# Folding the router's gate and noise weights into the MLP's second matrix, as 16 more columns, in place of transposes and products in the router

## The chip, the core and the metric

The kernel runs as one program on one core of a Trainium2 chip. The core has five engines that run their own instruction streams in order and meet only at semaphores: TensorE (PE, with its weight loads listed apart as PEld), VectorE (DVE), ScalarE (ACT), GpSimd (POOL) and SyncE (SP, which issues most DMA transfers). The metric is the device time of one execution in microseconds, as the median of several runs.

## The reference, cut to what matters

```python
# 1. linear attention over 3072 tokens: 4 batches x 8 heads x 768 steps, head size 48
state = alpha[t][:, None] * state + outer(k[t], v[t]);  y[t] = q[t] @ state
x = y as [3072, 384]
# 2. dense MLP
h = x @ w_in                       # [3072, 2048]
x = (h * sigmoid(h)) @ w_out       # [3072, 384]
# 3. mixture of experts, 8 experts, the best 2 for each token
logits = x @ w_gate;  noise_scale = log1p(exp(x @ w_noise))     # both [3072, 8]
noisy = logits + noise_scale * noise
# the two largest of noisy choose the experts, a softmax over the two weighs them
out[token] += weight * (relu(x[token] @ w1[e]) @ w2[e])
```

Since `x` of part 3 is `g @ w_out`, the two small products can also be written `g @ (w_out @ w_gate)` and `g @ (w_out @ w_noise)`. The change rests on that.

## The kernel before, in words

The program has three overlapping parts. The order of the instructions on each engine is the order in which the Python code issues them: nothing reorders them later.

**Attention** goes over 24 chunks of 128 tokens. `stage1_units` yields five units for a chunk: `unit_kt` with `unit_a` (transposes of k, products of k and q, masked on DVE into `am`), `unit_kv` (the state; DVE sums it in a tile `St` and scales it into `S`), two halves of `unit_y`, the second of which ends with the copy `xr` on ACT, and `unit_x` (transposes of `xr`, then `xh` on ACT and `xl` on DVE). Between them DVE prepares the next chunk (`prep_a`, `prep_b`, `prep_c`). All their PSUM tiles come from one pool `p1` with three buffers, name `ps1`, taken in turn.

**The MLP** goes over 8 blocks of 384 tokens (index `j`) and 16 slices of the hidden width (index `m`). `l1(j, m)` is 9 matmuls of 384 columns into a tile `ph`; `act1` makes `th` (ACT), `gf` (DVE), `gh` (ACT) and `gl`; `l2(j, m)` adds 9 matmuls into three accumulators `acc`, one for each 128 tokens. `l2` follows `l1` two iterations later (`LAG`). Matmuls run on pairs of high and low parts, three products for one. One attention unit is issued in each iteration, so the units of the first 15 yields stand alone at the start, and the other 105 lie between the MLP's matmuls.

**The MLP's weights** arrive in float64 halves. `narrow` turns a slice into float32 with three DVE instructions (lines 142 to 144) in a tile `wf` with three buffers, and `split` writes the high part on ACT (line 137) and the low part on POOL (line 138). `wn` and `wh` call them. Nine of the 32 slices are done in the first 15 units; in block 0 each iteration does two more, one of `wout` and one of `win`, until iteration 11. The high and low parts of `wout` are `wo_h` and `wo_l`.

**The router** of a block (`route(j)`) runs in steps between the iterations of the next block. For each of its three chunks it transposes the row of 384 values (3 PE transposes, line 96), copies them to `xt2` on ACT (line 531), multiplies by `wgn_t` (written as 3 matmuls of 16 columns, line 524; the trace counts 6) and copies the 16 sums beside the row (line 525). Then `gate` picks two experts on DVE, and POOL scatters the rows. The router of the last block runs in the first iterations of the expert part, which follows with its own matmuls (`e1`, `e2`).

Of the kernel before, what the change touches and what calls it, by code (L numbers as in the profile page):

```python
# [8 lines left out]
F32 = mybir.dt.float32  # L9
# [12 lines left out]
DM = H * D  # L22
# [32 lines left out]
def attention_mlp_moe(ctx: ExitStack, tc: tile.TileContext, aqk, vt, win, wout, wgn, noise, w12,  # L55
# [38 lines left out]
    def flip(o, x):  # L94
        n = x.shape[0]
        PE.transpose(o, x, ident[:n, :n])
# [21 lines left out]

    win_h = wpool.tile([128, MF, KD, 128], F32R)
    win_l = wpool.tile([128, MF, KD, 128], F32R)  # L120
    wo_h = wpool.tile([128, MF, DM], F32R)
    wo_l = wpool.tile([128, MF, DM], F32R)
    raw = {}

    def load_w(src, m):
# [10 lines left out]
    def split(h, l, r, eng=None):  # L136
        ACT.activation(h, r, AF.Copy)
        (eng or DVE).tensor_tensor(l, r, h.bitcast(F32), OP.subtract)
# [194 lines left out]
    def unit():  # L333
        next(gen, None)
# [19 lines left out]
    def wh(w):  # L354
        if w:
            (kind, m), f = w
            h, l = (win_h, win_l) if kind == "i" else (wo_h, wo_l)
            split(*[x[:, m].rearrange("p k j -> p (k j)") if kind == "i" else x[:, m] for x in (h, l)], f, POOL)

    wl(2)  # L360
    load_chunk(2)
# [5 lines left out]
    nc.scalar.dma_start(nz, noise)  # L367
    for i in range(15):
        unit()

    def range_load(i):
        raw["r", i] = load_w(win if i < MF else wout, i % MF)
# [69 lines left out]

    def l2(j, m):
        if m == 0:
            ACC[j] = [pa.tile([128, 512], F32, name=f"acc{i}")[:, :DM] for i in range(CPB)]
        gh, gl = GH.pop((j, m)), GL.pop((j, m))
        for i in range(CPB):
            sl = slice(i * C, (i + 1) * C)
            n = 0
            for g, w in ((gh, wo_h), (gh, wo_l), (gl, wo_h)):  # L450
                PE.matmul(ACC[j][i], g[:, sl], w[:, m], start=(m == 0 and n == 0),  # L451
                          stop=(m == MF - 1 and n == 2))
                n += 1
# [4 lines left out]
    def evac(j):  # L458
        rows[j] = r = rpool.tile([128, CPB, LGN], F32, name="row")
        for i in range(CPB):  # L460
            ACT.activation(r[:, i, :DM], ACC[j][i], AF.Copy, scale=0.5)
            if dbg is not None:
                c = j * CPB + i
                nc.sync.dma_start(dbg[c * C:(c + 1) * C], r[:, i, :DM])
# [52 lines left out]
    def route(j):  # L517
        c0 = j * CPB
        r = rows.pop(j)
        for i in range(CPB + 1):  # L520
            if i:
                p = p1.tile([128, 2 * E], F32, name="ps1")
                for k in range(KD):
                    PE.matmul(p, t[:, k], wgn_t[:, k], start=(k == 0), stop=(k == KD - 1))
                ACT.activation(r[:, i - 1, DM:], p, AF.Copy)
            if i < CPB:
                p = p1.tile([128, KD, 128], F32, name="ps1")
                for k in range(KD):
                    flip(p[:, k], r[:, i, k * 128:(k + 1) * 128])
                t = rpool.tile([128, KD, 128], F32, name="xt2")  # L530
                ACT.activation(t, p, AF.Copy)
            yield int(i < CPB) or None
        o, w, d = yield from gate(rpool, CPB, r[:, :, DM:DM + E], r[:, :, DM + E:], nz[:, c0:c0 + CPB])
        sel = rpool.tile([128, CPB, E], BF, name="sel")
        DVE.tensor_tensor(sel, o[:, :, 0], o[:, :, 1], OP.add)
        yield 1
        rk = p1.tile([128, CPB, E], F32, name="ps1")
        cb = cum[:, j % 2]
        PE.matmul(rk, tri, sel, start=True, stop=False)
        PE.matmul(rk, ones, cb[:, None, :].to_broadcast([128, CPB, E]), start=False, stop=False)  # L540
        for i in range(CPB - 1):
            n = CPB - 1 - i
            PE.matmul(rk[:, i + 1:], ones, sel[:, i:i + 1].to_broadcast([128, n, E]), start=False,
                      stop=i == CPB - 2)
        rs = rpool.tile([128, CPB, E], F32, name="rk")
        ACT.activation(rs, rk, AF.Copy)
        rk = rs
        cn = cum[:, (j + 1) % 2]
        DVE.tensor_reduce(cs, sel.rearrange("p c e -> p e c"), axis=AX.X, op=OP.add)
        DVE.tensor_tensor(cn, cb, cs, OP.add)  # L550
        DVE.tensor_copy(r[:, :, RW - 1].bitcast(I32), tok[:, c0:c0 + CPB])
        yield from gate_w(rpool, CPB, o, w, d, r[:, :, DM:DM + E])
        yield
        az, th = [rpool.tile([128, CPB, E], F32, name=x) for x in ("az", "rth")]
        ow = rpool.tile([128, CPB, 2, E], F32, name="ow")
        DVE.tensor_scalar(az, rk, float(CAP), 65536.0, op0=OP.is_ge, op1=OP.mult)
        DVE.tensor_tensor(th, rk, base, OP.add)
        DVE.tensor_tensor(th, th, az, OP.add)
        if j > PAST:
            DVE.tensor_scalar(az[:, :, :2], rk[:, :, :2], float(GRAB), 65536.0, op0=OP.is_lt, op1=OP.mult)  # L560
            DVE.tensor_tensor(th[:, :, :2], th[:, :, :2], az[:, :, :2], OP.add)
        DVE.tensor_tensor(ow, o, th[:, :, None, :].to_broadcast([128, CPB, 2, E]), OP.mult)
        pos = rpool.tile([128, CPB, 2], F32, name="pos")
        idx = rpool.tile([128, CPB, 2], I32, name="idx")
        DVE.tensor_reduce(pos, ow, axis=AX.X, op=OP.add)
        DVE.tensor_copy(idx, pos)
        yield
        scat[j] = []
        for i in range(CPB):
            for k in range(2):  # L570
                st = POOL.indirect_dma_start(
                    out=xd, out_offset=bass.IndirectOffsetOnAxis(ap=idx[:, i, k:k + 1], axis=0),
                    in_=r[:, i, :RW], in_offset=None, bounds_check=ROWS - 1, oob_is_err=False)
                for x in sum(scat.values(), []):
                    tc.declare_no_dep(st.ins, x.ins, reason="distinct rows")
                scat[j].append(st)
        assert bool(early) == (j > PAST)
        for st in scat[j]:
            for ld in early:
                tc.declare_no_dep(st.ins, ld.ins, reason="rows past those")  # L580
# [50 lines left out]
    for i in range(NS + LAG):  # L631
        if i < NS:
            j, m = divmod(i, MF)
            l1(j, m)
            if 12 <= i < 20:
                init_rows(i - 12, 8)
            if 32 <= i < 48 and i % 4 == 0:
                init_out(i // 4 - 8, 4)
            if 2 * MF <= i < 6 * MF:
                x = i - 2 * MF  # L640
                if x % 2 == 0:
                    range_load(x // 2)
                if x % 2 == 1 and x > 1:
                    range_check(x // 2 - 1)
            if i == 6 * MF:
                range_check(2 * MF - 1)
            if j == NB - 1:
                if m == 10:
                    okgen = ok_first()
                if m >= 10:  # L650
                    step(okgen)
                if m == 0:
                    s1c.close()
                    wev = w3c.enter_context(tc.tile_pool(name="wev", bufs=1, side="right"))
                    wst = w0c.enter_context(tc.tile_pool(name="wst", bufs=1, side="right"))
                    w3p[0], w3p["raw"] = wev, (wst, 2)
                if m == 1:
                    early = load_group(0, 0, wst, 4)
                if 8 <= m < 8 + len(GR[0][1]):
                    tr_tile(0, 0, m - 8)  # L660
                if m < 8:
                    w3_load(0, m)
                if m in (10, 11):
                    w3_load(1, m - 10)
                if 1 <= m < 9:
                    w3_split(0, m - 1)
            ac = act1(j, m)
            if j == 0:
                for _ in range(2):
                    w = wn()  # L670
                    step(ac)
                    wh(w)
                    step(ac)
            else:
                run(ac)
            if m < MF - 1 and j < NB - 1:
                unit()
        if i >= LAG:
            j, m = divmod(i - LAG, MF)
            l2(j, m)  # L680
            if m == MF - 1:
                evac(j)
            if m == 1 and j > 0:
                rgen = route(j - 1)
            for _ in range(LASTN if j == NB - 1 else 1 + (m >= RT2)):
                if rgen:
                    got = next(rgen, 0)
                    if got == 0:
                        rgen = None
                    if got == 1:  # L690
                        break
# [292 lines left out]
```

## Time and profile before

| what | value |
|---|---|
| median of 3 runs | 1103.37 us (1103.02 to 1105.49) |
| profiled execution, span from first to last instruction | 1103.1 us |
| PE busy | 1041.6 us, 94% of the span |
| DVE, ACT, POOL busy | 585.2, 399.6, 259.0 us |
| granted TensorE clock, mean | 0.987 |

The span and the median differ by 0.3 us. A PE that is 94% busy is not PE at its peak, since matmuls overlap and their ends are modelled. The share is also an average: in the first 130 us PE is busy less, and DVE more, than later. The sections below read those stages apart.

### The profile page before, as it was taken

The numbers are of one execution on the slowest core, as the hardware profiler recorded it, in microseconds if no ns is written. First come the engines' busy times: TensorE is split into PE (matmuls) and PEld (weight loads), VectorE is DVE, ScalarE is ACT, GpSimd is POOL, SyncE is SP. The second block draws the span as 40 slices with busy tenths as digits, with TensorE's granted clock in tenths as the row PEclk, the third lists the DMA queues.
The fourth block names the chain that finished last, engine by engine and source line by source line (L and its number), as shares of the span: only waits on it lengthen the run. The fifth ranks groups of instructions, "written<-read, shape, count | busy, mean of one in ns | idle before, by whom it ended". The sixth has DMA issues, their size and how long they took to land. (4 is left out here: it accounts for less than half of the span.)

```text
span 1103.1 us, 16832 instructions
## 1 busy us (share of the span) xinstructions
PE 1041.6 (94%) x6395; PEld 1006.9 (91%) x6395; DVE 585.2 (53%) x1319; ACT 399.6 (36%) x853; POOL 259.0 (23%) x252
## 2 busy tenths in 40 slices
PE   4678899999999999999999999999999999999995
PEld 3667799999999999999999998999999999999995
DVE  7889845657667676585646562244333333334220
ACT  3233343343433433334345431244333333333221
POOL 4455520310202102020020222211212122222212
PEclk9998899999999999999999999999999999999998
DMA  7344791533424224230032313545444344343212
GB/s 229 122 133 139 257 286 56 187 123 126 136 80 146 76 77 131 71 110 23 1 118 82 128 66 95 113 101 155 114 99 108 86 120 91 81 109 70 42 15 38
DMA packets 55225, 119.64 MB, mean 108 GB/s; under 512 B 6640, under 2 KB 33648, under 8 KB 55136
## 3 DMA queue, kind: packets, MB, share of 16 engines
q1 hardware_dynamic: 43456, 97.23, 28.4%
q0 software_dynamic: 11264, 20.68, 10.0%
q8 instruction: 52, 0.85, 0.3%
q10 hardware_dynamic: 416, 0.58, 0.2%
q14 instruction: 37, 0.30, 0.1%
HBM read 82.22 MB, written 36.24 MB: 107 GB/s over the span
## 5 line engine op out<-in xcount | busy, mean ns | idle before, releaser
L736 PE MATMUL acc<-w3h,hx 128*128 128x384 f32 x832 | 241.6, 342 | 1.9 <-ACT y L746 1.9
L717 DVE SCALAR_TENSOR_TENSOR hx<-ph,hx 128x64 fp32r<-128x64 f32 (+1 forms) x192 | 79.2, 443 | 295.6 <-ACT hx L713 293.0
L748 POOL DMA_INDIRECT out_dram<-y,xrow x64 | 98.5, 1539 | 335.0 <-ACT y L746 271.6
L713 ACT ACTIVATE hx<-ph 128x448 fp32r<-128x448 f32 (+1 forms) x128 | 65.5, 518 | 271.3 <-PE ph L710 191.8
L736 PEld LDWEIGHTS acc<-w3h,hx 128*128 128x128 f32 x832 | 153.1, 188 | 5.4 <-ACT y L746 2.2
L736 PE MATMUL acc<-w3l,hx 128*128 128x384 f32 x448 | 150.1, 335 | 0.0
L451 PE MATMUL acc<-wo_h,gh 128*128 128x384 f32 x384 | 139.5, 363 | 0.0
L710 PE MATMUL ph<-xh,w3h 128*128 128x384 f32 (+1 forms) x384 | 135.9, 354 | 0.8 <-DVE hx L717 0.8
L710 PE MATMUL ph<-xh,w3l 128*128 128x384 f32 (+1 forms) x384 | 135.1, 352 | 0.0
L710 PE MATMUL ph<-xl,w3h 128*128 128x384 f32 (+1 forms) x384 | 134.8, 351 | 0.0
L424 PE MATMUL ph<-xh,win_h 128*128 128x384 f32 x384 | 133.0, 346 | 1.2 <-DVE gf L434 0.6
L451 PE MATMUL acc<-wo_l,gh 128*128 128x384 f32 x384 | 130.1, 339 | 0.0
L451 PE MATMUL acc<-wo_h,gl 128*128 128x384 f32 x384 | 130.0, 339 | 0.0
L424 PE MATMUL ph<-xl,win_h 128*128 128x384 f32 x384 | 129.6, 337 | 0.0
L424 PE MATMUL ph<-xh,win_l 128*128 128x384 f32 x384 | 129.6, 337 | 0.0
L434 DVE SCALAR_TENSOR_TENSOR gf<-th,ph 128x384 f32<-128x384 f32 x128 | 70.5, 551 | 95.3 <-ACT th L431 84.6
L431 ACT ACTIVATE th<-ph 128x384 f32<-128x384 f32 x128 | 62.5, 488 | 134.7 <-PE ph L424 132.4
L439 ACT ACTIVATE gh<-gf 128x384 fp32r<-128x384 f32 x128 | 67.2, 525 | 112.3 <-DVE gf L434 108.6
L441 DVE TENSOR_TENSOR gl<-gf,gh 128x384 fp32r<-128x384 f32 x112 | 62.7, 559 | 66.3 <-ACT gh L439 62.8
L736 PEld LDWEIGHTS acc<-w3l,hx 128*128 128x128 f32 x448 | 81.1, 181 | 0.7
L451 PEld LDWEIGHTS acc<-wo_h,gh 128*128 128x128 f32 x384 | 73.6, 192 | 2.5
L710 PEld LDWEIGHTS ph<-xh,w3h 128*128 128x128 f32 x384 | 72.2, 188 | 3.8 <-DVE hx L717 1.1
(140 smaller groups left out, 1757.6 us busy)
## 6 DMA issues: line engine op xcount, KB each, us to landing
wraw<-in_w_dram SPq DMA_DIRECT2D x64, 384.0 KB
aqk<-in_aqk_dram SPq DMA_DIRECT2D x23, 674.2 KB
wraw<-in_win_dram SPq DMA_DIRECT2D x32, 384.0 KB
wraw<-in_wout_dram SPq DMA_DIRECT2D x32, 384.0 KB
xrow<-xd SPq DMA_DIRECT2D x48, 196.5 KB
xd<-pad SPq DMA_DIRECT2D x12, 589.5 KB
v<-in_v_dram SPq DMA_DIRECT2D x24, 192.0 KB
xd<-pad SPq DMA_DIRECT2D x4, 786.0 KB
```

What stands on the lines that cost most here:

```text
L424: PE.matmul(p, w[:, m, k], x[:, k], start=(n == 0), stop=(n == 3 * KD - 1))
L431: ACT.activation(th, p, AF.Tanh, scale=0.5)
L434: DVE.scalar_tensor_tensor(g, th, 1.0, p, op0=OP.add, op1=OP.mult)
L439: ACT.activation(gh, g, AF.Copy)
L441: (POOL if j == 0 else DVE).tensor_tensor(gl, g, gh.bitcast(F32), OP.subtract)
L451: PE.matmul(ACC[j][i], g[:, sl], w[:, m], start=(m == 0 and n == 0), stop=(m == MF - 1 and n == 2))
L710: PE.matmul(p[:, :N], w[:, k, fs], x[:, k], start=(n == 0), stop=(n == 3 * KD - 1))
L713: ACT.activation(hx[:, :N], p[:, :N], AF.Relu)
L717: DVE.scalar_tensor_tensor(hx[:, o:o + b - a], p[:, a:b], 0.0, hx[:, a:b].bitcast(F32), op0=OP.max, op1=OP.subtract)
L736: PE.matmul(AC3[e, g][t][:m], hx[:, o:o + m], w[:, f], start=(f == 0 and q == 0), stop=(f == FF - 1 and q == len(prods) - 1))
L748: st = POOL.indirect_dma_start(out=out, out_offset=bass.IndirectOffsetOnAxis(ap=x[:n, RW - 1:].bitcast(I32), axis=0), in_=y[a:a + n], in_o ...
```

## The change

Each slice of `wout`, once narrowed, is also multiplied by the gate and noise weights. `fold` transposes it (3 PE transposes), copies the result on ACT into a tile of the name `St`, multiplies by `wgn_t` on PE, copies the 16 columns into `wo_h` on ACT and subtracts into `wo_l` on DVE. It runs after units 5, 10 and 15 (for one, two and one slices), and once at the head of each iteration 1 to 12 of block 0, behind that iteration's `l1`. The matmuls of `l2` become 400 columns wide, the accumulators are copied with 400 columns, and the router loses its transposes and products.

```diff
-    wo_h = wpool.tile([128, MF, DM], F32R)
-    wo_l = wpool.tile([128, MF, DM], F32R)
+    wo_h = wpool.tile([128, MF, LGN], F32R)
+    wo_l = wpool.tile([128, MF, LGN], F32R)
...
+            if kind == "o":
+                folds.append((m, f))
+    folds = []
+    def fold():
+        while folds:
+            m, f = folds.pop(0)
+            p = p1.tile([128, KD, 128], F32, name="ps1")
+            for k in range(KD):
+                flip(p[:, k], f[:, k * 128:(k + 1) * 128])
+            t = s1.tile([128, KD, 128], F32, name="St", bufs=1)
+            ACT.activation(t, p, AF.Copy)
+            p = p1.tile([128, 2 * E], F32, name="ps1")
+            for k in range(KD):
+                PE.matmul(p, t[:, k], wgn_t[:, k], start=(k == 0), stop=(k == KD - 1))
+            ACT.activation(wo_h[:, m, DM:], p, AF.Copy)
+            DVE.tensor_sub(wo_l[:, m, DM:], p, wo_h[:, m, DM:].bitcast(F32))
...
     for i in range(15):
         unit()
+        if i % 5 == 4:
+            fold()
...
-            ACC[j] = [pa.tile([128, 512], F32, name=f"acc{i}")[:, :DM] for i in range(CPB)]
+            ACC[j] = [pa.tile([128, 512], F32, name=f"acc{i}")[:, :LGN] for i in range(CPB)]
...
-            ACT.activation(r[:, i, :DM], ACC[j][i], AF.Copy, scale=0.5)
+            ACT.activation(r[:, i], ACC[j][i], AF.Copy, scale=0.5)
...
     def route(j):
         c0 = j * CPB
         r = rows.pop(j)
-        for i in range(CPB + 1):
-            if i:
-                p = p1.tile([128, 2 * E], F32, name="ps1")
-                for k in range(KD):
-                    PE.matmul(p, t[:, k], wgn_t[:, k], start=(k == 0), stop=(k == KD - 1))
-                ACT.activation(r[:, i - 1, DM:], p, AF.Copy)
-            if i < CPB:
-                p = p1.tile([128, KD, 128], F32, name="ps1")
-                for k in range(KD):
-                    flip(p[:, k], r[:, i, k * 128:(k + 1) * 128])
-                t = rpool.tile([128, KD, 128], F32, name="xt2")
-                ACT.activation(t, p, AF.Copy)
-            yield int(i < CPB) or None
...
             ac = act1(j, m)
             if j == 0:
+                fold()
                 for _ in range(2):
```

On DVE, at the head of iteration 4 of block 0 (behind the second `unit_y` of a chunk), the order before is this: the last instruction of a narrowing, `prep_c`'s product, the next narrowing, and `gf`.

```order
L144 SCALAR_TENSOR_TENSOR wf<-wraw,wf 128x384
L226 TENSOR_TENSOR aqk<-aqk,R 112x512
L142 TENSOR_SCALAR wf<-wraw 128x384
L143 SCALAR_TENSOR_TENSOR wf<-wraw,wf 128x384
L144 SCALAR_TENSOR_TENSOR wf<-wraw,wf 128x384
L434 SCALAR_TENSOR_TENSOR gf<-th,ph 128x384
```

In the changed kernel the same place on DVE reads as follows (line 376 is the fold's subtraction, line 454 the old line 434).

```order
L144 SCALAR_TENSOR_TENSOR wf<-wraw,wf 128x384
L226 TENSOR_TENSOR aqk<-aqk,R 112x512
L376 TENSOR_TENSOR wo_l<-ps_764,wo_h 128x16
L142 TENSOR_SCALAR wf<-wraw 128x384
L143 SCALAR_TENSOR_TENSOR wf<-wraw,wf 128x384
L144 SCALAR_TENSOR_TENSOR wf<-wraw,wf 128x384
L454 SCALAR_TENSOR_TENSOR gf<-th,ph 128x384
```

The subtraction now stands between one narrowing and the next. On ACT, at the same place, the order before is the split of `win`, the copy `xr`, and the next iteration's `th`, split and `gh`.

```order
L137 ACTIVATE win_h<-wf 128x384
L282 ACTIVATE xr<-ps_593 128x384
L431 ACTIVATE th<-ph 128x384
L137 ACTIVATE wo_h<-wf 128x384
L439 ACTIVATE gh<-gf 128x384
```

In the changed kernel ACT has the fold's two copies there (lines 371 and 375; line 451 is the old 431, line 459 the old 439).

```order
L137 ACTIVATE win_h<-wf 128x384
L282 ACTIVATE xr<-ps_665 128x384
L371 ACTIVATE St<-ps_758 128x384
L375 ACTIVATE wo_h<-ps_764 128x16
L451 ACTIVATE th<-ph 128x384
L137 ACTIVATE wo_h<-wf 128x384
L459 ACTIVATE gh<-gf 128x384
```

Both copies now stand ahead of `th`. On PE, at the same place, before: the last two matmuls of `l1(0, 4)`, the transposes of `unit_x`, and `l2(0, 2)`.

```order
L424 MATMUL ph<-xl,win_h 128x384
L424 MATMUL ph<-xh,win_l 128x384
L96 MATMUL ps_700<-ident,xr 128x128 x3
L451 MATMUL acc_600<-wo_h,gh 128x384
L451 MATMUL acc_600<-wo_l,gh 128x384
```

In the changed kernel (line 444 is the old 424, line 471 the old 451):

```order
L444 MATMUL ph<-xl,win_h 128x384
L444 MATMUL ph<-xh,win_l 128x384
L96 MATMUL ps_758<-ident,wf 128x128 x3
L374 MATMUL ps_764<-wgn_t,St 128x16 x3
L96 MATMUL ps_796<-ident,xr 128x128 x3
L471 MATMUL acc_672<-wo_h,gh 128x400
```

The products of line 374, which need ACT's copy, now stand ahead of the unit and of `l2` on PE.

## Rows read from the trace of the kernel before

**Rows 1.** Busy time by stage: window, length, PE, PEld, DVE, ACT, POOL, PEclk, DMA, GB/s.

```profile
55.00:130.00 75.00, 57.48 (x328) 54.28 (x329) 66.89 (x101) 27.22 (x60) 39.61 (x37) 0.89 0.50 158
...
200.00:300.00 100.00, 99.08 (x676) 96.85 (x675) 67.77 (x166) 39.31 (x90) 21.34 (x25) 1.00 0.43 146
```

**Rows 2.** Timeline of PE round two router steps of block 1: start, duration, what.

```profile
237.75 0.34 PE L451 MATMUL acc<-wo_h,gl 128*128 128x384 f32 x1
...
239.05 0.34 PE L424 MATMUL ph<-xl,win_h 128*128 128x384 f32 x1
...
243.56 0.34 PE L451 MATMUL acc<-wo_h,gl 128*128 128x384 f32 x1
244.41 0.84 PE L524 MATMUL ps<-wgn_t,xt 128*128 128x16 f32 x6 [0.51 <-ACT kts L235]
...
245.72 0.34 PE L424 MATMUL ph<-xl,win_h 128*128 128x384 f32 x1
```

**Rows 3.** Who waited for whom, PE: total us, times, longest us.

```profile
PE ps L524 <- ACT kts L235: 3.3, 6, 0.8
```

**Rows 4.** Timeline of PE, 27 matmuls of 384 columns, then 9 of 448.

```profile
619.07 0.33 PE L451 MATMUL acc<-wo_h,gh 128*128 128x384 f32 x1
...
623.75 0.36 PE L710 MATMUL ph<-xh,w3h 128*128 128x448 f32 x1
...
625.40 0.36 PE L710 MATMUL ph<-xh,w3l 128*128 128x448 f32 x1
```

**Rows 5.** Timeline of PE, ACT and DVE at the end of chunk 0.

```profile
23.65 0.90 PE L96 MATMUL ps<-ident,xr 128*128 128x128 f32 x3 [3.31 <-ACT xr L282]
24.59 0.49 ACT L294 ACTIVATE xh<-ps 128x384 fp32r<-128x384 f32 x1 [0.99 <-PE ps L96]
25.59 1.22 DVE L205 TENSOR_TENSOR_SCAN P<-aqk,past 112x516 f32<-112x516 f32 x1
```

**Rows 6.** Timeline of ACT behind the router's products of Rows 2.

```profile
245.29 0.18 ACT L525 ACTIVATE row<-ps 128x16 f32<-128x16 f32 x1 [0.93 <-PE ps L524]
```

**Rows 7.** Timeline of DVE in block 0, where an iteration's first narrowing begins, and gf.

```profile
98.98 0.35 DVE L142 TENSOR_SCALAR wf<-wraw 128x384 int32<-128x384 int32 x1
...
110.70 0.56 DVE L144 SCALAR_TENSOR_TENSOR wf<-wraw,wf 128x384 int32<-128x384 int32 x1
111.18 0.35 DVE L142 TENSOR_SCALAR wf<-wraw 128x384 int32<-128x384 int32 x1
...
112.16 1.25 DVE L144 SCALAR_TENSOR_TENSOR wf<-wraw,wf 128x384 int32<-128x384 int32 x1
114.31 0.56 DVE L434 SCALAR_TENSOR_TENSOR gf<-th,ph 128x384 f32<-128x384 f32 x1 [0.89 <-POOL gl L441]
...
117.16 0.35 DVE L142 TENSOR_SCALAR wf<-wraw 128x384 int32<-128x384 int32 x1
...
119.98 0.54 DVE L434 SCALAR_TENSOR_TENSOR gf<-th,ph 128x384 f32<-128x384 f32 x1
...
124.15 0.41 DVE L142 TENSOR_SCALAR wf<-wraw 128x384 int32<-128x384 int32 x1
```

**Rows 8.** Timeline of ACT in block 0, the last instruction ahead of th.

```profile
97.74 0.52 ACT L235 ACTIVATE kts<-ps 128x448 f32<-128x448 f32 x1
...
111.30 0.53 ACT L137 ACTIVATE win_h<-wf 128x384 fp32r<-128x384 f32 x1 [1.65 <-DVE wf L144]
...
117.10 0.47 ACT L282 ACTIVATE xr<-ps 128x384 f32<-128x384 f32 x1
...
123.17 0.47 ACT L294 ACTIVATE xh<-ps 128x384 fp32r<-128x384 f32 x1
```

**Rows 9.** Timeline of PE at the end of block 0's preparation.

```profile
130.88 0.36 PE L275 MATMUL ps<-S,aqk 112*128 112x96 f32 x2
...
141.78 0.45 PE L96 MATMUL ps<-ident,xr 128*128 128x128 f32 x2 [0.49 <-ACT xr L282]
```

**Rows 10.** Timeline of ACT, th of iteration 11 of block 0.

```profile
131.12 0.47 ACT L431 ACTIVATE th<-ph 128x384 f32<-128x384 f32 x1
```

**Rows 11.** Busy time by stage, columns as in Rows 1, behind an idle PE.

```profile
117.60:122.20 4.60, 4.58 (x16) 4.58 (x17) 4.50 (x6) 1.34 (x3) 3.05 (x3) 0.50 0.53 149
```

More of the change, by code (lines that the diff above doesn't have):

```diff
@@ L357, in wh @@
             h, l = (win_h, win_l) if kind == "i" else (wo_h, wo_l)
-            split(*[x[:, m].rearrange("p k j -> p (k j)") if kind == "i" else x[:, m] for x in (h, l)], f, POOL)
+            split(*[x[:, m].rearrange("p k j -> p (k j)") if kind == "i" else x[:, m, :DM] for x in (h, l)], f, POOL)
+            if kind == "o":
[14 more added lines that the diff above has]
+            DVE.tensor_sub(wo_l[:, m, DM:], p, wo_h[:, m, DM:].bitcast(F32))
     wl(2)
```

## Prediction, made before the changed kernel was run

> **What bounds the kernel now.** I read the busy times by stage first. From 200 us on PE is busy 99.08 of 100 us [rows 1]; the reader should see that DVE and ACT have room there, so a microsecond of PE is a microsecond of the result. From 55 to 130 us it is otherwise: DVE is busy 66.89 of 75 us and PE 57.48 [rows 1]. There DVE narrows 23 weight slices and prepares attention chunks; PE has gaps, and what makes DVE wait moves everything behind it. So the change takes work from the stage where PE is full, and adds work where DVE is.
>
> **What the router gives back.** I read the timeline of PE round its steps. Between the last `l2` matmul ahead of a step and the second `l1` matmul behind it lie 1.30 us (237.75 to 239.05) [rows 2]. Two starts of plain 384-column matmuls take 2 x 0.1733 us: the 27 starts from 619.07 to 623.75 take 4.68 us [rows 4]. So products and transposes for one chunk cost 1.30 - 0.35 = 0.95 us, and 24 chunks cost 22.9 us. In six blocks one step takes 2.16 us (243.56 to 245.72) [rows 2]: its products wait for a PSUM buffer that ACT's `kts` holds. The view of waits counts six [rows 3]. The excess of 2.16 over 1.30 is 0.86 us, six times 5.2 us. `route` has then no use of `p1` until its ranks, and the next unit that wants the buffer comes an `l1` later, so I take the wait to vanish. Sum: **-28.1 us**. If those waits come back elsewhere it is -22.9.
>
> **What the wider `l2` costs.** Eight starts of 448 columns, 623.75 to 625.40, take 0.206 us each, against 0.1733 for 384 [rows 4]: 0.033 us for 64 columns, 0.0081 for 16. In proportion to columns it would be 0.0072. After the head below, 116 of the 128 `l2` calls are left, 1044 matmuls: **+8.5 us** (7.5 by the lower price).
>
> The Trainium skill (page "TensorE: Matmul & The Clock Gate", section "Back-to-back issue gap") gives one matmul N / 2.4 + 2.5 ns, thus 6.7 ns for 16 columns and, as an estimate, 7.0 us for the 1044. The rows put 384 columns at 173 ns where the page's formula has 162.5, so I keep the rows.
>
> **What the folds cost.** The transposes and products of a fold are cheap on PE. Its chain is not: transposes on PE, copy `t` on ACT, products on PE, copy on ACT, subtraction on DVE. All are written at one place, and each engine runs in order, so DVE stands at the subtraction (line 376) until the chain is through. Behind it queue the next narrowing, the splits on ACT and POOL that need it, and `gf`. PE stands at the products until ACT has reached `t`.
>
> The chain from the start of `t`: the copy takes 0.49 us (as `xh`) [rows 5]; a PE start behind ACT some 0.06; from products that had to wait to ACT's copy 0.88 us (244.41 to 245.29) [rows 2, 6], that copy 0.18 [rows 6], and about 0.17 for the start and occupancy of a 16-column DVE instruction. Together 1.78 us.
>
> *The first 15 units, four folds.* PE runs there at half its later pace: three transposes reach ACT after 0.94 us (23.65 to 24.59) [rows 5], where two later ones last 0.45 [rows 9], so three about 0.56. I lengthen the products in the same ratio, 0.88 to 1.48. `t` can start when `xh` ends, about 25.1; the chain ends at 25.1 + 0.49 + 0.06 + 1.48 + 0.18 + 0.17 = 27.5. DVE now goes on at 25.59 [rows 5], so it stops for 1.9 us. Two of the three places have one fold; that with two repeats transposes, copy and products in series, some 2.8 us more. Sum 1.9 + 4.7 + 1.9 = 8.5 us.
>
> *Block 0, iterations 1 to 10.* The unit ahead of a fold decides how long DVE stops, and each of five kinds comes twice.
> - Behind `unit_kt`: the fold's transposes need the PSUM buffer that `kts` frees at 98.26 [rows 8]. 98.26 + 0.56 + 1.78 = 100.6 against DVE's 98.98 [rows 7]: 1.6 us.
> - Behind `unit_kv`: `t` shares the tile `St`, which DVE's own last instruction reads. The whole chain lies behind it: 1.8 us.
> - Behind the first `unit_y`: 111.83 [rows 8] + 1.78 - 111.18 [rows 7] = 2.4 us.
> - Behind the second: the transposes need the buffer that `xr` frees at 117.57 [rows 8]; + 0.56 + 1.78 - 117.16 [rows 7] = 2.8 us.
> - Behind `unit_x`: 123.64 [rows 8] + 1.78 - 124.15 [rows 7] = 1.3 us.
>
> Twice their sum is 19.8 us. Part is given back. The third instruction of a narrowing takes 0.56 us at 110.70 and 1.25 at 112.16 [rows 7], while POOL works on its splits. While DVE stops at a fold POOL gets them done, and the narrowing behind it should run alone, about 1.5 us from its start to `gf`. Now that takes 3.13 us behind the first `unit_y` (111.18 to 114.31, with a wait of 0.89 for POOL) and 2.82 behind the second (117.16 to 119.98) [rows 7]. So 1.6 and 1.3 us come back, and I put the kinds with one or two long instructions at 1.1 (`unit_kv`), 0.7 (`unit_x`) and 0 (`unit_kt`). Twice the sum is 9.4 us: net 10.4. Since PE sometimes reaches its transposes late I add 0.6 (0 to 1.2).
>
> The Trainium skill (page "SBUF — State Buffer", section "Who interferes with whom") says that a DVE instruction with two SBUF inputs and a GpSimd instruction that reads SBUF exclude each other, whichever starts first. The long and short narrowings agree with it. By it POOL's work done in the stop is wholly given back; if nothing came back the sum would be 9.4 us higher.
>
> *Iterations 11 and 12.* PE now runs ahead of ACT; with the folds it can't. In iteration 11 ACT is free for `t` at 131.12 [rows 10], so the products start at 131.7 and end near 132.4. Then come, in PE's order, `l2` (1.7), `l1` (1.56), transposes (0.56), the wait for `t` (0.55) and products (0.66), near 137.4. Before, from the place behind that `l1` (130.88) to the transposes of `unit_x` (141.78, of it 0.49 us of wait) [rows 9], PE took 10.4 us. I put 1.2 of that to waits for DVE, which leaves 9.2, and add 0.15 for wider matmuls. So it gets there at 146.7 in place of 141.78: 4.9 us. From there PE is full and keeps the delay.
>
> Head: 8.5 + 10.4 + 0.6 + 4.9 = **+24.4 us**.
>
> Costed at nothing: the wider copies of the accumulators and the router's copies that fall away, since ACT is busy 39 of 100 us there [rows 1] (uncovered, the 48 copies that go would be worth less than 48 x 0.5 us of ACT, in the other direction); and the last block's scatter, three steps earlier, for which only later loads wait. No DMA issue is added or moved past another.
>
> **Sum.** -28.1 + 8.5 + 24.4 = +4.8 us on the profiled 1103.1, thus 1107.9; the median lies 0.3 us above the span: **1108.2 us**, slower by 0.4%. A measurement of this kernel can tell about 0.2%, 2.2 us.
>
> **The rivals.**
> 1. *The folds hide* (faster). If DVE were not the bound where they stand, only 16 subtractions of some 0.13 us would show: 1103.4 + 2.1 + 8.5 - 28.1 = 1086 us. For it: PE has 17 us without work from 55 to 130 us [rows 1]. Against it: DVE has but 8. It decides once all the head's delays are under 28.1 - 8.5 - 2.2 = 17.4 us; partly hidden, it gives 1086 to 1100.
> 2. *PE falls to its lower clock in the waits for `t`, or POOL's time isn't given back* (slower still). Behind an idle stretch the granted clock was 0.50, 1.2 GHz, for 4.6 us [rows 11]. If that followed every wait of block 0, products would last 0.6 us longer, 12 x 0.6 = 7.2 us: 1115. Without POOL's 9.4 us: 1118. Against it: PE now does in each iteration what it did ahead, so its gaps get shorter. The Trainium skill (page "TensorE: Matmul & The Clock Gate", section "HAM oscillation — how this bites in real kernels") warns that gaps between bursts bring the clock down each time; rows 11 show one such stretch.
> 3. *The change leaves `l2` as it was*: if 16 columns cost nothing, 1099.7. The 448-column rows speak against it, and I give it no chance of its own.
>
> **Chances.** Forecast 0.53, with its own range 1101 to 1115, of which 0.35 slower, 0.14 within 0.2%, 0.04 faster. Rival 1: 0.28, of it 0.25 faster and 0.03 the same. Rival 2: 0.19, all slower. So faster 0.29, same 0.17, slower 0.54. The range of 1095 to 1117 leaves out half of rival 1 and a third of rival 2, 0.2 together.
>
> **What would show it.** Right: no products of line 524, no wait for `kts` by the router, `l2` starts 0.181 us apart; DVE idle ahead of line 376 on ACT, 1.3 to 2.8 us each in block 0, longer in the first 55 us; PE full from about 146 + 20 us on. Wrong: little idle time ahead of line 376; the transposes of chunk 5's `unit_x` near 150 us rather than 166; the granted clock of PE low between 60 and 150 us; or gaps of PE that return in blocks 1 to 7.

## The result

The changed kernel takes 1118.4 us (median of 4), the one before 1103.6: a ratio of 1.0131, 95% interval 1.0116 to 1.0145. The profiled execution has a span of 1116.5 us, 13.4 longer than before. (The medians differ by 14.8: this run's time, 1118.28 us, lies 1.8 us above its span, where the span before lies 0.3 under its median, so the execution profiled before was probably one of the longer ones.) The forecast had the sign, not the size: 1118.4 lies above its 1108.2 and above its upper end of 1117.

The stages first. Busy time by stage in the changed kernel, columns as in [rows 1]:

```profile
55.00:130.00 75.00, 59.09 (x309) 55.03 (x309) 50.77 (x92) 26.45 (x63) 29.66 (x30) 0.85 0.37 109
...
200.00:300.00 100.00, 100.00 (x678) 97.98 (x677) 70.27 (x187) 38.44 (x87) 18.63 (x22) 1.00 0.42 136
```

From 200 us PE has no gap left: the router's waits for `kts` are gone. From 55 to 130 us DVE, which was busy 66.89 of 75 us [rows 1], is busy 50.77: it stands. Who waited for whom, DVE and then PE (total us, times, longest us):

```profile
DVE wo_l L376 <- ACT wo_h L375: 35.0, 16, 4.8
...
PE ps L374 <- ACT St L371: 20.0, 16, 4.8
...
PE ph L718 <- DVE hx L725: 3.5, 1, 3.5
```

Sixteen folds, 35.0 us of DVE standing at the subtraction. The last line is new and lies in the expert stage.

The wider `l2`, timeline of PE in the changed kernel:

```profile
252.34 0.34 PE L471 MATMUL acc<-wo_l,gh 128*128 128x400 f32 x1
...
253.80 0.33 PE L444 MATMUL ph<-xh,win_h 128*128 128x384 f32 x1
...
618.42 0.34 PE L471 MATMUL acc<-wo_l,gh 128*128 128x400 f32 x1
...
619.86 0.33 PE L444 MATMUL ph<-xh,win_h 128*128 128x384 f32 x1
```

Eight starts of 400 columns take 1.46 us in one place and 1.44 in another, 0.180 to 0.183 each, against 0.1733 [rows 4]; the prediction had 0.181.

**Where the head grew.** The transposes of chunk 5's `unit_x`, 141.78 before [rows 9], now begin at 172.65, 30.9 us later, where 24.4 were predicted; 0.54 us of it is the first input of this execution, which came later (DVE's first scan at 6.29, against 5.75). The copies of block 0's accumulators mark the end of the head; timelines of ACT before and in the changed kernel:

```profile
155.02 1.25 ACT L461 ACTIVATE row<-acc 128x384 f32<-128x384 f32 x3
...
186.04 1.36 ACT L481 ACTIVATE row<-acc 128x400 f32<-128x400 f32 x3
```

They begin 31.0 us later. Five stops of DVE in a row, one behind each kind of unit (timeline of DVE, in brackets the wait ahead of line 376):

```profile
117.87 0.17 DVE L376 TENSOR_TENSOR wo_l<-ps,wo_h 128x16 fp32r<-128x16 f32 x1 [2.13 <-ACT wo_h L375]
...
126.98 0.17 DVE L376 TENSOR_TENSOR wo_l<-ps,wo_h 128x16 fp32r<-128x16 f32 x1 [2.38 <-ACT wo_h L375]
...
135.92 0.17 DVE L376 TENSOR_TENSOR wo_l<-ps,wo_h 128x16 fp32r<-128x16 f32 x1 [4.66 <-ACT wo_h L375]
...
142.68 0.17 DVE L376 TENSOR_TENSOR wo_l<-ps,wo_h 128x16 fp32r<-128x16 f32 x1 [1.85 <-ACT wo_h L375]
...
149.47 0.17 DVE L376 TENSOR_TENSOR wo_l<-ps,wo_h 128x16 fp32r<-128x16 f32 x1 [0.97 <-ACT wo_h L375]
```

They stand behind `unit_kt`, `unit_kv`, the first and the second `unit_y`, and `unit_x`. The third, 4.66 us, is about twice the forecast's 2.4. The timelines of ACT, then PE, and PE's busy time by stage show how it comes about:

```profile
124.72 0.49 ACT L371 ACTIVATE St<-ps 128x384 f32<-128x384 f32 x1 [1.99 <-DVE S L264]
126.76 0.18 ACT L375 ACTIVATE wo_h<-ps 128x16 fp32r<-128x16 f32 x1 [1.55 <-PE ps L374]
...
134.28 0.49 ACT L371 ACTIVATE St<-ps 128x384 f32<-128x384 f32 x1 [2.47 <-PE ps L96]
135.71 0.18 ACT L375 ACTIVATE wo_h<-ps 128x16 fp32r<-128x16 f32 x1 [0.93 <-PE ps L374]
```

```profile
125.26 1.46 PE L374 MATMUL ps<-wgn_t,St 128*128 128x16 f32 x6 [3.25 <-ACT St L371]
...
129.12 0.68 PE L471 MATMUL acc<-wo_h,gh 128*128 128x400 f32 x1
...
132.13 0.34 PE L444 MATMUL ph<-xh,win_h 128*128 128x384 f32 x1
...
133.70 0.49 PE L96 MATMUL ps<-ident,wf 128*128 128x128 f32 x3
134.83 0.84 PE L374 MATMUL ps<-wgn_t,St 128*128 128x16 f32 x6 [0.64 <-ACT St L371]
...
138.59 0.34 PE L444 MATMUL ph<-xh,win_h 128*128 128x384 f32 x1
```

```profile
125.26:131.90 6.64, 6.64 (x26) 6.62 (x27) 4.14 (x8) 2.08 (x5) 2.34 (x4) 0.50 0.20 63
132.13:136.86 4.73, 4.09 (x32) 3.82 (x31) 0.91 (x3) 1.06 (x3) 1.74 (x2) 1.00 0.27 83
```

`t` shares the tile `St` with `unit_kv`, so ACT waits for DVE's last use of it, and PE stands 3.25 us at the products. Behind that wait PE runs 6.64 us at a granted clock of 0.50, the 1.2 GHz level: its products, the unit and nine `l2` matmuls (129.12 to 132.13, 3.0 us where 1.6 would do). From the products to the end of `l2` that makes 6.87 us (125.26 to 132.13); the same sequence at the next fold, at a granted clock of 1.00, takes 3.76 (134.83 to 138.59). So the next fold's transposes come only at 133.70, when ACT has long been free, and DVE stands until 135.92. The same happened one chunk earlier (DVE's stops of 2.38 and 4.79 us). The low clock also shows in the stop behind `unit_kv` itself: from the start of the products to ACT's copy it takes 1.50 us here (125.26 to 126.76) and 0.88 at the next fold (134.83 to 135.71).

**The expert stage.** It takes 480.4 us (636.09 to 1116.5) where it took 479.35 (623.75 to 1103.1), though three router steps of 0.95 us are gone from it. Timelines of SP, ACT and PE in the changed kernel:

```profile
636.28 1.77 SPq L612 DMA_DIRECT2D xrow<-xd  x4
638.09 0.60 SPq L614 DMA_DIRECT2D xrow<-xd  x1
638.73 2.01 SPq L594 DMA_DIRECT2D wraw<-in_w_dram  x4
663.07 1.98 SPq L612 DMA_DIRECT2D xrow<-xd  x3
665.16 0.84 SPq L594 DMA_DIRECT2D wraw<-in_w_dram  x2
```

```profile
669.84 0.84 ACT L137 ACTIVATE w3h<-wraw 128x768 fp32r<-128x768 f32 x1 [10.01 <-DMA wraw<-in_w_dram]
```

```profile
672.41 0.71 PE L718 MATMUL ph<-xh,w3h 128*128 128x448 f32 x1 [3.46 <-DVE hx L725]
```

SP issues four of expert 1's weight loads, then stands at the load of the third group's rows (line 612) until the last block's scatter is through at 663, and only then issues the last two weight loads. ACT waits 10.01 us for them and PE 3.46. Before, all six weight loads went out in a row from 626.39 on, and the load for which SP stands came behind them. Timeline of SP before:

```profile
626.39 13.21 SPq L587 DMA_DIRECT2D wraw<-in_w_dram  x6
663.11 4.71 SPq L605 DMA_DIRECT2D xrow<-xd  x8
```

### The profile page after: what moved, and what is told of

Read it like the earlier page. It is cut to its first block, busy times and chain, and to the rows that moved or that the text cites. A ratio compares the mean times of both kernels' runs of the same rounds, so it can differ in the third digit from the quotient of the medians.

```text
span 1116.5 us, 16697 instructions
## 1 busy us (share of the span) xinstructions
PE 1055.8 (95%) x6323; PEld 1020.6 (91%) x6323; DVE 586.5 (53%) x1335; ACT 395.1 (35%) x837; POOL 260.0 (23%) x252
## 5 line engine op out<-in xcount | busy, mean ns | idle before, releaser
L471 PE MATMUL acc<-wo_h,gh 128*128 128x400 f32 x384 | 143.7, 374 | 0.0
L471 PE MATMUL acc<-wo_l,gh 128*128 128x400 f32 x384 | 134.3, 350 | 0.0
L471 PE MATMUL acc<-wo_h,gl 128*128 128x400 f32 x384 | 134.1, 349 | 0.0
L461 DVE TENSOR_TENSOR gl<-gf,gh 128x384 fp32r<-128x384 f32 x112 | 72.3, 646 | 66.3 <-ACT gh L459 61.6
```

The costliest lines, as they stand in the source:

```text
L461: (POOL if j == 0 else DVE).tensor_tensor(gl, g, gh.bitcast(F32), OP.subtract)
```

## The experiments

Theory: the missing 10 us are DVE's stops, mis-sized behind `unit_kv` and at the fold after it, and a load that overtook the weight loads. Rivals: the 16 columns cost more than their share, or the router gave back less.

**One part at a time.** `cols_only` is the kernel before with 400-column products; the 16 more columns are the next slice's, and nobody reads them:

```diff
-    PE.matmul(ACC[j][i], g[:, sl], w[:, m], ...)
+    PE.matmul(ACC[j][i], g[:, sl], w[:, m * DM:m * DM + LGN], ...)
```

> The kernel before with one thing of the change: the second layer's products are 400 columns wide (the 16 more are the next slice's first columns, or zeros, and nobody reads them); router and everything else stay as they were. The prediction's term (1044 matmuls off the first block's hidden part, 0.0081 us each) gives +8.5 us, so 1112. If the pitch that rows of the changed kernel show (9 starts in 1.62 to 1.66 us, against 1.56) holds in all of them, 116 groups of nine cost 7 to 11.5 us: 1110.5 to 1115. If wider products cost nothing (the prediction's third rival): 1103.6.

Measured: 1111.6, ratio 1.0070 (1.0056 to 1.0083): +8.0 us. The forecast's price holds.

`folds_only` is the kernel before with the folds written to a small tile that nobody reads:

```diff
+            ACT.activation(wxh, p, AF.Copy)
+            DVE.tensor_sub(wxl, p, wxh.bitcast(F32))
```

> The kernel before with the folds alone: the same transposes, copies, products and the DVE subtraction at the same places, written to a small tile that nobody reads; the products stay 384 wide and the router does its own products. The prediction's head of 24.4 us gives 1128. The head of about 28 us that the changed kernel's trace shows by the sixth chunk's last unit gives 1131.7. If folds hid behind other work (first rival): 1103.6 to 1106.

Measured: 1134.3, ratio 1.0274 (1.0260 to 1.0288): +30.7 us, where the forecast had 24.4. Timeline of ACT in this run:

```profile
186.06 1.27 ACT L482 ACTIVATE row<-acc 128x384 f32<-128x384 f32 x3
```

Block 0's accumulators are copied out from 186.06, as in the changed kernel (186.04). The folds alone make the head; products and router have no part in it.

**The load.** `load_behind` issues that one load behind the weight loads:

```diff
-                        load_group(*groups[2], k3, 12)
...
+            if i == 6:
+                load_group(*groups[2], k3, 12)
```

> The changed kernel, in which only the load of the third group's rows is issued later in SP's queue, behind the last loads of expert 1's weights, as it stood before the change. If that load, waiting for the last block's scatter, held the weight loads back (ACT idle 10.0 us ahead of w3h, PE 3.5 us for hx, part of it at a lower clock), the time falls by 3 to 4.5 us, to 1114 to 1115.5, and PE's 3.5 us wait is gone. If the weights were late for another reason, it stays at 1118.4.

Measured: 1112.7, ratio 1.0076 (1.0062 to 1.0090), 5.75 us under the changed kernel. SP in that run:

```profile
639.44 15.00 SPq L594 DMA_DIRECT2D wraw<-in_w_dram  x6
663.80 4.43 SPq L612 DMA_DIRECT2D xrow<-xd  x8
```

All six weight loads are out first, and PE's wait for `hx` is gone. More came back than the wait, and than the 3 to 4.5 us expected: from 660 to 680 us the granted clock was 0.83 in the changed kernel and is 1.00 here. Part of it is no harm of the change. The kernel before had a wait and a slow stretch in this place too (timeline of PE before; the granted clock was 0.57 from 668 to 672 us):

```profile
667.50 0.44 PE L736 MATMUL acc<-w3h,hx 128*128 128x384 f32 x1 [1.88 <-ACT y L746]
```

The expert stage took 479.35 us before, thus 476.5 without three router steps of 0.95; it takes 480.4 in the changed kernel and 474.5 in `load_behind` (636.80 to 1111.3). By these traces the overtaking load costs 3.9 us, and 2.0 us more come from a stage that runs better than before.

**The shared tile.** `own_tile` gives `t` a tile of its own:

```diff
-            t = s1.tile([128, KD, 128], F32, name="St", bufs=1)
+            t = s1.tile([128, KD, 128], F32, name="wt3", bufs=1)
-            k = s1.tile([C, NP, PR], F32, name="kts")
+            k = s1.tile([C, NP, PR], F32, name="kts", bufs=1)
```

> The changed kernel, in which the transposed weights get a tile of their own, where they shared St with the state update of unit_kv (kts gets by with one buffer, which gives the room). If only the wait for that tile is saved (ACT 1.99 us at 124.72, 2.6 us one chunk before): 4 to 5 us less, 1113.5 to 1114.5. If that wait is also why PE then runs at the lower clock, and so why the next fold's stop lasts 4.66 us and not 2.3: 8 to 10 us less, 1108.5 to 1110.5. If PE is late anyway and the shared tile is an accident: 1117 to 1118.4.

Measured: 1114.3, ratio 1.0099 (1.0085 to 1.0112): 4.1 us less. Behind `unit_kv` DVE no longer waits, and the two long stops shrink from 4.79 and 4.66 to 2.98 and 2.08 (timeline of DVE):

```profile
92.12 0.17 DVE L376 TENSOR_TENSOR wo_l<-ps,wo_h 128x16 fp32r<-128x16 f32 x1 [2.98 <-ACT wo_h L375]
...
129.54 0.17 DVE L376 TENSOR_TENSOR wo_l<-ps,wo_h 128x16 fp32r<-128x16 f32 x1 [2.08 <-ACT wo_h L375]
```

All stops together fall from 35.0 us to 26.7, 8.4 less, but block 0's copies start only 5.1 us earlier (180.97 against 186.04, and 0.3 of that is the start): the rest was given back. So the time falls on the first forecast (4 to 5 us), while the next fold's stop shrinks as in the second. The lower clock isn't gone with the wait: PE still runs at 0.50 from 82.2 to 88.7 us, there close behind a wait of 1.34 us, and one later stop grows from 1.85 to 2.87. How much of the long stops was the wait itself and how much the clock behind it, this run doesn't part; nor does it show what the single buffer of `kts` costs.

**Who stands.** `pool_sub` leaves each fold in its place, but POOL does the subtraction from a copy in SBUF:

```diff
-            ACT.activation(wo_h[:, m, DM:], p, AF.Copy)
-            DVE.tensor_sub(wo_l[:, m, DM:], p, wo_h[:, m, DM:].bitcast(F32))
+            x = s1.tile([128, 2 * E], F32, name="wgx", bufs=1)
+            ACT.activation(x, p, AF.Copy)
+            ACT.activation(wo_h[:, m, DM:], x, AF.Copy)
+            POOL.tensor_tensor(wo_l[:, m, DM:], x, wo_h[:, m, DM:].bitcast(F32), OP.subtract)
```

> The changed kernel with each fold where it was, but DVE has no part in it: ACT copies the 16 columns once more to a small SBUF tile, and POOL, which is not full in the first block, does the subtraction. If the cost is DVE standing at that subtraction (35.0 us of waits in the changed kernel, of which some is given back), the head's 30.7 us fall to 6 or less: 1091 to 1095. If ACT's copy of the transposed weights and the products hold up ACT and PE in the same place, so that th and then gf come late for DVE instead, half or less is saved: 1101 to 1112.

Measured: 1107.1, ratio 1.0026 (1.0015 to 1.0036): 11.3 us less, under half of the head. DVE now stands at `gf` instead. In the first 175 us it waited there for `th` 13.4 us in the kernel before, and here:

```profile
DVE gf L456 <- ACT th L453: 27.2, 10, 4.7
```

So the theory that DVE's subtraction alone is at fault falls: ACT and PE stand in the fold too, and `th` is behind them. (The one more copy on ACT may be part of what is left; it wasn't tested apart.)

**Spreading the fold.** `spread` cuts it in two, each piece where its inputs should be there already. `fold_a` is the transposes and ACT's copy, to a tile of its own; `fold_b` is the products, ACT's copies and the subtraction on POOL. In block 0:

```diff
-                fold()
-                for _ in range(2):
+                for k in range(2):
                     w = wn()
                     step(ac)
                     wh(w)
+                    if k == 0:
+                        fold_b()
                     step(ac)
...
+        if i < MF:
+            fold_a()
```

In the first 15 units both stand behind each unit. `spread_load` adds the edit of `load_behind`.

> The changed kernel with the fold in two pieces: the transposes and ACT's copy of them (to a tile of its own; kts gets by with one buffer) at the end of an iteration, behind the second layer's products; the products behind the next iteration's first-layer products, ACT's copies behind its next weight split, and the subtraction on POOL. In the first 15 units the two pieces stand behind two successive units. If the round trip PE, ACT, PE, ACT, DVE in one place is the cost, the head of 30.7 us falls to 2 to 6: 1090 to 1094 (1118.4 - 30.7 + 2 to 6). If the work itself fills an engine that bounds the first block (PE is at 59 of 75 us there, ACT at 26), 10 us or more of the head stay: 1098 or more.

> The same with the load of the third group's rows behind the last weight loads of expert 1, as in the run that showed 5.75 us for it. If the two causes add up, 5 to 6 us below the run without this edit: 1084 to 1089, and PE's wait for hx in the expert stage is gone.

Measured: `spread` 1104.7, ratio 1.0006 (0.9996 to 1.0015); `spread_load` 1099.6, ratio 0.9963 (0.9952 to 0.9973). The load is worth 5.1 us here too, so the two causes add up. But block 0's copies still began at 175.08, 20 us later than in the kernel before, which I had not expected; by the recorded expectation (1098 or more) it spoke for the other reading, that the added work itself fills an engine. Timeline of PE in `spread`, first 60 us:

```profile
22.98 0.88 PE L96 MATMUL ps<-ident,wf 128*128 128x128 f32 x3 [4.17 <-DVE wf L144]
36.64 0.90 PE L96 MATMUL ps<-ident,wf 128*128 128x128 f32 x3 [2.30 <-DVE wf L144]
55.54 0.90 PE L96 MATMUL ps<-ident,wf 128*128 128x128 f32 x3 [2.30 <-DVE wf L144]
```

The transposes now stood too early: PE waited for a slice that DVE had not yet narrowed, with the next unit queued behind. Two more versions move the transposes one step later, and the second keeps the pieces of the first 15 units off the chain `unit_y`, `xr`, `xh`, scan.

`spread2` in block 0, where both pieces take slices of earlier iterations:

```diff
                     step(ac)
+                    if k == 0:
+                        ready += folds
+                        folds.clear()
+                        fold_b()
+                        fold_a()
                     wh(w)
-                    if k == 0:
-                        fold_b()
                     step(ac)
```

`spread3`, besides, turns one slice at a time, and in the first 15 units:

```diff
-        while ready:
+        if ready:
...
         unit()
-        fold_b()
-        fold_a()
+        if i % 5 in (4, 0, 1):
+            fold_b()
+            fold_a()
```

> The run before this with the fold's transposes one step later, so that no engine meets a weight slice that DVE has just begun to narrow (there PE waited 9.1 us in four places for wf, the longest 4.2): in the first block behind the next iteration's first-layer products, its own products another iteration later, both ahead of ACT's weight split; in the first 15 units one unit later. If these early waits are what was left of the head (evacuation of block 0 at 175.1, 20 us behind the kernel before), some 10 us go: 1088 to 1092. If PE's and ACT's added work itself holds th and so gf back: 1096 to 1099.6.

> The same, and in the first 15 units the pieces stand only behind unit_x and the first two units of the next chunk, none on the chain from unit_y over xr and xh to the next chunk's scan. If that chain sets the first 15 units (scans P at 25.59 and 40.68 before, 28.4 and 47.3 in the spread run), 4 to 8 us less than the run beside it. If DVE's own work sets them, the same time.

Measured: `spread2` 1090.7, ratio 0.9888 (0.9872 to 0.9905); `spread3` **1087.7, ratio 0.9861 (0.9844 to 0.9877)**, the best of all. `spread2` took 8.9 us off `spread_load` (8.3 by the two ratios), so most of what was left of the head came from pieces that stood too early, not from the added work. `spread3` took 3.0 more, less than the 4 to 8 expected. Busy time by stage in `spread3`, columns as in [rows 1], and its timeline of ACT at the end of block 0:

```profile
55.00:130.00 75.00, 65.88 (x399) 62.44 (x398) 66.25 (x100) 34.24 (x89) 44.62 (x47) 0.84 0.52 154
```

```profile
161.11 1.36 ACT L491 ACTIVATE row<-acc 128x400 f32<-128x400 f32 x3
```

DVE is as full as before, 66.25 of 75 us against 66.89 [rows 1], and PE has taken up the folds beside it, 65.88 against 57.48. Block 0's copies begin 6.1 us later than in the kernel before; at the scan of chunk 6 it is 1.2 us (130.24 against 129.01), so what is left arises in the last iterations, where PE is full (busy 31.00 of 31 us from 130 to 161).

**The router by itself.** `router_kept` is `spread3` with the old router steps put back and the fold's outcome unread:

> The best version so far with the router's own transposes and products put back, as in the kernel before: the products stay 400 columns wide (the 16 more are read by nobody), the folds stay spread as they are but go to a small tile that nobody reads, the third group's load stands where it stood before. The difference to that version (1087.7) is what the router's removal gives by itself. The prediction's sum of 28.1 us gives 1115.8; 22.9 us, if the waits for kts had come back elsewhere, 1110.6; the remainder of the runs so far (30.7 + 8.0 + 5.75 - 14.85 = 29.6 us) gives 1117.3.

Measured: 1116.7, ratio 1.0115 (1.0097 to 1.0132). The difference to `spread3` is 29.0 us, or 28.0 by the two ratios.

## Why the prediction failed

| term | predicted | measured |
|---|---|---|
| router gone | -28.1 | -29.0 (28.0 by ratios) |
| 16 more columns in `l2` | +8.5 | +8.0 |
| head: folds | +24.4 | +30.7 |
| order of loads on SP | 0 | +5.75 (3.9 by the traces) |
| sum | +4.8 | +15.45 (13.6 with 3.9; the kernel itself: +14.8) |

Each measured term is a difference of two medians, so the sum can be off by a few us.

Right were the router's return and the price of a column. The six waits for `kts` are gone as forecast; what they were worth by themselves, no run separates.

Two steps failed. **The first is "No DMA issue is added or moved past another".** The router's removed steps were also what held back, by three rounds of the expert loop, the load that is issued when `route` ends. Nothing in the diff touches a DMA; but the load now goes out ahead of two weight loads, and since it waits for the scatter, SP's queue stands with it. Taking that load back is worth 5.75 us, shown by `load_behind`, of which about 3.9 are harm done by the change.

**The second is the size of a term of the head**, the stop behind the first `unit_y`. By stretches, from the trace after less that before: first 15 units 8.8 (predicted 8.5); iterations 1 to 10 of block 0 15.4 (11.0); the end of the block 6.3 (4.9). In iterations 1 to 10 the ten stops and subtractions sum to 24.5 where 19.8 were predicted. Behind `unit_kt` they are 1.68 and 2.13 (predicted 1.6), `unit_kv` 2.38 twice (1.8), first `unit_y` 4.79 and 4.66 (2.4), second 1.86 and 1.85 (2.8), `unit_x` 0.94 and 0.97 (1.3); each subtraction adds 0.09, which the predicted figures include. Given back were 24.5 - 15.4 = 9.1 us, predicted 9.4. I had seen that `t` shares `St`, and priced the wait for the fold that meets it, not for the next one: I let that one start when ACT is free (111.83 + the shift), but PE reached its transposes late. The 0.6 us set aside for that was 4.65 (4.79 + 4.66 - 2 x 2.4). The two stops behind `unit_kv` are longer by what their products took more at the lower clock (1.50 us to ACT's copy, where the prediction had 0.88). `own_tile` shows the shared tile as the cause of both, but for a rest: without it the stops behind `unit_kv` are gone and the two long ones come down to 2.98 and 2.08, 4.1 us of time in all. What made the block's end 1.4 us longer I did not separate.

What came back can be seen in the narrowings. Over iterations 0 to 10 of block 0 their 66 DVE instructions took 48.5 us before and 40.7 in the changed kernel: 21 of them lasted over 0.9 us before, 11 after. DVE's two waits for POOL's `gl`, 1.8 us together, are gone as well. Behind the long stop, where POOL had no work until 138.18, the instruction that took 1.25 us at 112.16 [rows 7] reads:

```profile
136.99 0.56 DVE L144 SCALAR_TENSOR_TENSOR wf<-wraw,wf 128x384 int32<-128x384 int32 x1
```

The Trainium skill (page "SBUF — State Buffer", section "Who interferes with whom") has a DVE instruction with two SBUF inputs and a GpSimd instruction that reads SBUF exclude each other; the short and long narrowings agree.

Rival 2 forecast 1115 to 1118 and comes near by its number, in part by luck. What POOL did in the stops was given back, against its second half, and the load on SP is in no rival. Of the clock it had the products right (0.6 us more behind `unit_kv`), but not every wait did it: in iterations 1 to 10 stretches at 0.50 follow PE's waits of 4.85, 3.25, 1.99 and 1.98 us, and none follows those of 0.58 to 0.96. From 132.13 to 136.86 the clock was 1.00 though PE had stood 0.64 us at a fold. From 55 to 130 us the mean clock hardly fell, 0.85 against 0.89 [rows 1]; but two of the slow stretches now lie where the next fold waits. The Trainium skill (page "TensorE: Matmul & The Clock Gate", section "HAM oscillation — how this bites in real kernels") warns of gaps between bursts: the stretches at 0.50 agree, the shortest gaps here show none of it.

Rival 1, that folds hide, was a matter of where they stand: as written they put off block 0's copies by 31.0 us, in `spread3` by 6.1.

## What to carry to other kernels

- A piece of work whose parts go round several in-order queues (PE, ACT, PE, ACT, DVE) stops each of them when it is written in one place. Written in pieces, each behind the step by which its input is surely there, nearly the same work put the end of the block off by 6 us instead of 31. Too early costs as well: with pieces ahead of their input it was 20.
- Removing steps from a generator moves all that is issued when it ends. Look at the order of each DMA queue after a change that touches no DMA.
- When one stop is priced, price the next one with the lateness that the first leaves on every engine.

## Unexpected on the hardware

Taking away a wait of 3.46 us of PE in the expert stage saved 5.75 in the end: the granted clock was 0.66 from 668 to 678 us behind it, and 1.00 in the same stage of `load_behind`. And DVE's stops cost less than their sum, 15.4 us for 24.5 in iterations 1 to 10, since most of its narrowings behind a stop ran faster while POOL had no work (0.56 us against 1.25).
